# A first-layer product ahead of the counts, and the second block's rows fetched earlier and turned later

## The chip, the cores and the metric

One core of a Trainium2 chip runs the whole program. The metric is the time of one execution in device microseconds; the median of three runs is given, and the profile is of one execution of its own.

## What is computed

Three layers follow one another on 2304 tokens (4 batches of 576) of width 512: a causal attention with a decay, a mixture of eight experts in which each token goes to one expert, and a gated layer. The change lies at the seam of the first two. The reference of these, cut to what matters:

```python
def _attn_ref(q, k, v, f):                     # 4 batches, 8 heads, 576 tokens, width 64
    scores = scale * np.matmul(q, k.transpose(0, 1, 3, 2))
    cum = np.cumsum(np.log(np.clip(f, 0.0001, 1.0)), axis=-1)
    scores = np.where(causal, -1000000000.0, scores + cum[:, :, :, None] - cum[:, :, None, :])
    attn = np.exp(scores - np.max(scores, axis=-1, keepdims=True))
    return np.matmul(attn / (np.sum(attn, axis=-1, keepdims=True) + 1e-09), v)

def _moe_ref(x, w_gate, w_output_gate, w1, w2):
    logits = x @ w_gate
    e_idx = np.argmax(logits, axis=1)          # the one expert of a token
    ...                                        # gate_w: its probability; eom: a sigmoid gate
    for e in range(E):
        mask = e_idx == e
        h = np.maximum(x[mask] @ w1[e], 0.0)
        out[mask] = gate_w[mask, None] * eom[mask, e, None] * (h @ w2[e])
```

## The kernel before

**Attention.** Sixteen pairs of heads (four pairs for each of four batches) are worked on one after another. Every operation of this stage is added to a planner (Flow) with a cost in ns, the engines that may do it, what it reads and writes, and a group, which is the number of its pair. The planner walks a modelled time, takes on each engine the ready operation that can start first and, among equals, that of the earliest group, and emits the instructions in the order so found. In finish (line 444) a pair's output is multiplied by a matrix that holds an identity and the two gates' weights: the product px (L451) has 80 columns for each head, 64 of x and 16 shares of the logits. VectorE scales it by the inverse sums into xb (scale, L461). After the last pair of a batch, logits (line 570) adds the last two heads' shares (L585), and route (line 589) takes the argmax (first, L609 to L614), counts the tokens of each expert by products with a triangle and with ones (prefix, L620 to L625, into the px buffer), works out each token's place in its expert's list (place), and the gate weight (weight, L650). Then the rows, with all 80 columns of 8 heads, are scattered to x_d in DRAM by POOL's indirect DMAs (scatter, L665), five for a batch.

**Before the last batch is known.** While the last pair runs, ahead_rows (line 702) and ahead_steps (line 740) already fetch and turn 216 rows of the expert that leads after three batches, and load and split three of its weight tiles. Every operand of an expert product is split in two: a high half by a cast (ScalarE) and a low half by a subtraction (VectorE); a product is then three matmuls.

**The expert steps.** The function moe (line 996) runs blocks of tokens: block 0 holds those 216 rows, block 1 the next 128 rows of the same expert, block 2 and further the other experts, of up to 336 rows. Each block has eight steps, one for each 128 of the 1024 hidden columns; all steps together are numbered s, so that block 1 begins with step 8 and block 2 with step 16. A step has first products (hidden, L1069, 12 matmuls), a ReLU with its split (relu, L1075 and L1076), and second products (down, L1101 to L1103 or, for 128 rows, L1088 to L1090), which are issued one step later, behind the next step's first products. At a block's end down copies its four outputs (put, L984 and L986: two by ScalarE, two by VectorE). Weight tiles come by SP's DMAs (load, L1014) into a ring of three raw buffers, and split (L1019 and L1020) splits tile s + 2 during step s; load s + 4 is issued in step s, once the split of tile s + 1 has freed its buffer. Rows of the next block are fetched by SP (fetch, L1031), which waits for all scatters, scaled by their gate weight (weigh, L1041 on ScalarE for block 1, L1043 on POOL after that), turned on TensorE (turn, L1053) and split (land, L1057 and L1058). For block 1 the order was: fetch behind load 8 in step 4, weigh at the end of step 6's ReLU, turn and land in step 7, ahead of the second products of step 6 and of the split of tile 9. From here on no planner is at work: each engine has its instructions in the order in which the code issues them, and SP its DMAs.

## Time and profile before

| | us |
|---|---|
| median of 3 runs | 880.24 (880.14 to 880.37) |
| the profiled execution | 880.27 |
| its span, from the first to the last instruction | 878.5 |
| TensorE busy | 851.4 (97% of the span) |
| VectorE busy | 613.2 (70%) |
| ScalarE busy | 451.3 (51%) |
| POOL busy | 316.3 (36%) |

The engines are PE (TensorE), PEld (its weight loads), DVE (VectorE), ACT (ScalarE), POOL and SP, which only issues DMAs here (SPq is its sequencer). L1069 is line 1069 of the kernel. A timeline's row has the start in us from the span's start, the length of the merged stretch, the engine, the line, the operation, out<-in, the shapes and the count; in brackets stands the idle time of the engine before it and what ended that. PEclk is the granted clock of TensorE as a share of 2.4 GHz, averaged over the stretch.

### The profile page before, as it was taken

What the parts mean: (1) busy time and instruction counts of PE and PEld (TensorE: products, weight loads), DVE (VectorE), ACT (ScalarE), POOL (GpSimd) and SP (SyncE); (2) the same over time, 40 slices, a digit from 0 to 9 for tenths busy, and PEclk for the clock granted to TensorE, in tenths of its full rate; (3) what the DMA queues carried; (4) which work ended last, traced back from release to release, by engine and by line L of the source; (5) the groups of instructions that cost most, each with busy time, mean ns of one, the idle gap of its engine ahead of it and who ended that gap; (6) DMA issues with size and microseconds to landing.
All of it is one profiled execution on the core that took longest, in us unless ns stands there. A gap on an engine that the chain in (4) does not pass through costs nothing.

```text
span 878.5 us, 16055 instructions
## 1 busy us (share of the span) xinstructions
PE 851.4 (97%) x5668; PEld 748.8 (85%) x5668; DVE 613.2 (70%) x1435; ACT 451.3 (51%) x990; POOL 316.3 (36%) x382
## 2 busy tenths in 40 slices
PE   7999999998999999999999999999999999999996
PEld 3766667666999999999999898999999989999995
DVE  5777787796675767757747788989898866344444
ACT  5878778785464455546555544353444432332220
POOL 4211233240222231233155346565646285322213
PEclk9999999999999999999999999999999999999999
DMA  7798969552688676687655557777774666655631
GB/s 218 210 294 266 272 195 286 160 175 96 225 265 298 215 249 223 200 298 251 191 175 183 176 187 166 199 149 207 133 185 130 186 227 240 231 205 206 216 131 72
DMA packets 84693, 179.89 MB, mean 205 GB/s; under 512 B 10097, under 2 KB 47473, under 8 KB 83073
## 3 DMA queue, kind: packets, MB, share of 16 engines
q1 hardware_dynamic: 81057, 168.19, 62.2%
q0 software_dynamic: 3552, 10.63, 3.2%
q8 instruction: 46, 0.75, 0.4%
q14 instruction: 38, 0.31, 0.1%
HBM read 123.89 MB, written 54.90 MB: 204 GB/s over the span
## 4 chain that ended last, share of the span: by engine, by line
PE 71%; DVE 9%; DMA 8%; ACT 4%; issue 4%; POOL 3%; SPq 1%; POOLq 0%; ACTq 0%; DVEq 0%
PE po L1505 12%; PE ph L1069 12%; PE w L1415 6%; PE x L1415 6%; PE z L1415 6%; PE py L1101 4%; PE py L1103 4%; PE py L1102 4%; PE y L1415 3%; PE tp L474 3%; PE ps L487 3%; DMA q<-in_qT 2%; PE po L512 2%; PE px L451 1%; DMA k<-in_kT 1%
## 5 line engine op out<-in xcount | busy, mean ns | idle before, releaser
L1433 POOL TENSOR_TENSOR s<-s,s 128x384 f32<-128x384 f32 x36 | 42.9, 1191 | 130.8 <-ACT s L1432 130.7
L1415 PE MATMUL x<-xo,wt 128*128 128x384 f32 x432 | 88.1, 338 | 1.7 <-DVEq L928 0.7
L1415 PE MATMUL z<-xo,wt 128*128 128x384 f32 x432 | 87.1, 335 | 1.9 <-DVE r L1475 1.9
L1415 PE MATMUL w<-xo,wt 128*128 128x384 f32 x432 | 86.7, 335 | 0.3 <-DVE r L1476 0.3
L427 ACT ACTIVATE sc<-sc,nmx 128x512 f32<-128x512 f32 (+3 forms) x128 | 71.7, 563 | 21.6 <-DVE nmx L422 20.7
L1415 PEld LDWEIGHTS x<-xo,wt 128*128 128x128 f32 x432 | 76.5, 188 | 6.4 <-ACT s L1426 1.0
L1415 PEld LDWEIGHTS z<-xo,wt 128*128 128x128 f32 x432 | 76.0, 188 | 3.2 <-DVE r L1475 2.8
L1043 POOL TENSOR_SCALAR xg<-xr 128x512 f32<-128x512 f32 (+5 forms) x20 | 34.9, 1754 | 117.2 <-DMA xr<-x_d 117.2
L1415 PEld LDWEIGHTS w<-xo,wt 128*128 128x128 f32 x432 | 75.9, 188 | 0.6 <-DVE r L1476 0.6
L1238 POOL TENSOR_TENSOR tt<-tt 128x256 f32<-128x256 f32 x48 | 40.2, 849 | 69.0 <-DVE tt L1205 67.6
L1505 PE MATMUL po<-wo,g1h 128*128 128x512 f32 x204 | 64.3, 397 | 0.0
L1426 ACT COPY s<-x 128x384 f32<-128x384 f32 x36 | 17.3, 481 | 90.6 <-PE x L1415 74.4
L345 ACT COPY pt<-tp 128x512 f32<-128x512 f32 (+3 forms) x128 | 50.0, 423 | 14.3 <-PE tp L474 14.1
L474 PE MATMUL tp<-ident,sc 128*128 128x128 f32 x320 | 52.9, 287 | 3.6 <-ACT ptz L345 2.1
L474 PEld LDWEIGHTS tp<-ident,sc 128*128 128x128 f32 x320 | 35.5, 142 | 21.2 <-ACT pt L345 6.5
L487 PE MATMUL ps<-k,q 64*128 64x512 f32 (+3 forms) x256 | 47.1, 476 | 5.7 <-DMA k<-in_kT 5.7
L1511 DVE TENSOR_TENSOR acc<-po,acc 128x512 f32<-128x512 f32 x60 | 39.9, 685 | 16.5 <-PE po L1505 15.8
L422 DVE CUSTOM_DVE_ANT_0 sc<-ps,cm 128x128 f32<-128x128 f32 x128 | 33.2, 285 | 19.6 <-PE tp L474 8.9
L1505 PEld LDWEIGHTS po<-wo,g1h 128*128 128x128 f32 x204 | 38.2, 188 | 7.7
L422 DVE CUSTOM_DVE_ANT_0 sc<-ps,cb,nmx 128x384 f32<-128x384 f32 (+2 forms) x96 | 43.6, 479 | 0.5
L1415 PE MATMUL y<-xo,wt 128*128 128x384 f32 x216 | 43.2, 334 | 0.0
L512 PE MATMUL po<-pt,vt 128*64 128x256 f32 (+1 forms) x384 | 42.1, 350 | 0.0
(334 smaller groups left out, 2436.3 us busy)
## 6 DMA issues: line engine op xcount, KB each, us to landing
raw<-in_w SPq DMA_DIRECT2D x69, 512.0 KB
w_d<-wt SPq DMA_DIRECT2D x84, 256.0 KB
wt<-w_d SPq DMA_DIRECT2D x12, 1792.0 KB
raw<-in_wm SPq DMA_DIRECT2D x18, 1024.0 KB
cb<-cum_d SPq DMA_DIRECT2D x30, 288.0 KB
x_d<-roomf SPq DMA_DIRECT2D x8, 960.0 KB
w_d<-wo SPq DMA_DIRECT2D x24, 256.0 KB
wo<-w_d SPq DMA_DIRECT2D x6, 1024.0 KB
```

The source lines that it names most:

```text
L345: self.nc.scalar.copy(out, in_)
L422: nc.vector.tensor_tensor_reduce(out=sc.t[:, cs], in0=ps.t[:, o:o + w], in1=in1(), scale=-0.125, scalar=acc if c else 3e38, op0=ALU.add, o ...
L427: F.add(lambda e: nc.scalar.activation(sc.t[:, :n], sc.t[:, :n], AF.Exp, bias=nmx.t[:, u:u + 1], scale=-1.0, accum_out=sums.t[:, u:u + 1]) ...
L474: nc.tensor.transpose(tp.t[:n, c - c0], sc.t[:, c * P:c * P + n], self.ident)
L487: nc.tensor.matmul(ps[j].t[:, :ext], lhsT=q.t[h, q0 + 64 * j:q0 + 64 * j + P], rhs=k.t[h, :ext], start=True, stop=True)
L512: nc.tensor.matmul(po.t[64 * j:64 * j + 64, o:w], lhsT=vt.t[:, c, (2 * p + j) * D:(2 * p + j + 1) * D], rhs=at[j].t[:, c, o:w], start=c == ...
L1069: nc.tensor.matmul(ph[:, :n], lhsT=a, rhs=b, start=i == 0, stop=i == len(mm) - 1)
L1238: nc.gpsimd.tensor_tensor(out=ts[:, o], in0=ts[:, a], in1=ts[:, b], op=ALU.subtract)
L1415: nc.tensor.matmul(bank, lhsT=l, rhs=r, start=first and not k and not i, stop=end and k == HK - 1 and i == 2, skip_group_check=True)
L1433: nc.gpsimd.tensor_tensor(out=s5, in0=s5, in1=s7, op=ALU.add)
L1505: nc.tensor.matmul(po, lhsT=a, rhs=b, start=i == 0, stop=i == len(mm) - 1)
L1511: nc.vector.tensor_tensor(out=acc[i], in0=po, in1=acc[i], op=ALU.add)
```

## The change

Step 0's first products become operations of the planner (ahead_hidden), which depend on the last pair's three px products and so come behind them, and have the group of the pair before; its ReLU goes with them, and step 0 of moe has only its second products left. The counts go into the po buffer instead of px. For tiles 0 and 1 of the last pair VectorE scales only the 16 logits' columns of each head; the 64 columns of x are scaled by four ScalarE instructions that the planner puts behind the argmax. In the last batch the logits' additions are done for tiles 2 to 4 and for tiles 0 and 1 apart. In moe the fetch of block 1's rows is issued ahead of load 8; weigh comes behind step 7's ReLU; turn comes behind the second products of step 6, then those of step 7 follow at once, and then land.

```diff
--- before.py
+++ after.py
@@ -450,20 +450,32 @@
                     for h in range(0, n, 64):
                         nc.tensor.matmul(px.t[h:h + 64, i], lhsT=oT.t[:, i * P + h:i * P + h + 64], rhs=self.w2[:, p],
                                          start=True, stop=True)
-            F.add(turn_x, {"PE": 272 * len(ts)}, r=[oT, "w2"], w=[px], group=pr, kind="x", mode="columns")
+            F.add(turn_x, {"PE": 272 * len(ts)}, r=[oT, "w2"], w=[px, ("px", pr, ts[0])], group=pr,
+                  kind="x", mode="columns")
             o = xb[:n, ts[0]:ts[-1] + 1, 2 * p:2 * p + 2, :]
-            x = px.t[:n, 0:len(ts)].rearrange("p t (j c) -> p t j c", j=2)
             w = [("xb", b % 2, p, t) for t in ts]
             if ts[0] < 4:
                 u = [2 * TORD.index(t) + j for t in ts for j in range(2)]

-                def scale(e):
+                def scale(e, cs=slice(0, XW)):
                     nc.vector.tensor_tensor(
-                        out=o, in0=x, op=ALU.mult, in1=rs.t[:, u[0]:u[-1] + 1].rearrange(
-                            "p (t j) -> p t j", j=2).unsqueeze(3).to_broadcast([P, len(ts), 2, XW]))
-                F.add(scale, {"DVE": 70 + 166 * len(ts)}, r=[px] + [(rs, i) for i in u], w=w, group=pr, kind="scale")
+                        out=o[..., cs], in0=px.t[:n, 0:len(ts)].rearrange("p t (j c) -> p t j c", j=2)[..., cs], op=ALU.mult,
+                        in1=rs.t[:, u[0]:u[-1] + 1].rearrange(
+                            "p (t j) -> p t j", j=2).unsqueeze(3).to_broadcast([P, len(ts), 2, cs.stop - cs.start]))
+                ready = [px] + [(rs, i) for i in u]
+                if pr == NP - 1 and ts[0] == 0:
+                    F.add(lambda e: scale(e, slice(D, XW)), {"DVE": 140}, r=ready, w=w + [("xl", b % 2, t) for t in ts], group=pr, kind="scale")
+
+                    def others(e):
+                        for i in range(len(ts)):
+                            for j in range(2):
+                                nc.scalar.activation(o[:, i, j, 0:D], px.t[:n, i, j * XW:j * XW + D], AF.Copy,
+                                                     scale=rs.t[:, u[0] + 2 * i + j:u[0] + 2 * i + j + 1])
+                    self.rest = lambda ohb: F.add(others, {"ACT": 800}, r=ready + [ohb], w=w, group=pr, kind="scale")
+                else:
+                    F.add(scale, {"DVE": 70 + 166 * len(ts)}, r=ready, w=w, group=pr, kind="scale")
             else:
-                F.add(lambda e: self.copy(e, o, x), {"ACT": 190, "DVE": 240}, r=[px], w=w, group=pr, kind="x")
+                F.add(lambda e: self.copy(e, o, px.t[:n, 0:len(ts)].rearrange("p t (j c) -> p t j c", j=2)), {"ACT": 190, "DVE": 240}, r=[px], w=w, group=pr, kind="x")

         def turn(sc, c0, c1, n, out, key):

@@ -581,9 +593,12 @@
                 {"DVE": 570}, r=got, w=[lg], group=pr)
         elif p == NPB - 1:
             lg = self.lg
-            for h in (H - 2, H - 1):
-                F.add(lambda e, h=h: nc.vector.tensor_tensor(out=lg.t, in0=lg.t, in1=xb[:, :, h, D:], op=ALU.add),
-                      {"DVE": 155}, r=got + [lg], w=[lg], group=pr)
+            for t0, t1 in ((2, 5), (0, 2)) if b == B - 1 else ((0, 5),):
+                ready = [("xl", b % 2, t) if b == B - 1 and not t0 else ("xb", b % 2, p, t) for t in range(t0, t1)]
+                for h in (H - 2, H - 1):
+                    F.add(lambda e, h=h, t0=t0, t1=t1: nc.vector.tensor_tensor(
+                        out=lg.t[:, t0:t1], in0=lg.t[:, t0:t1], in1=xb[:, t0:t1, h, D:], op=ALU.add),
+                        {"DVE": 130}, r=ready + [lg], w=[lg], group=pr)
             self.route(b, pr)

     def route(self, b, pr):
@@ -593,7 +608,7 @@
         xb, lg = self.xb[b % 2], self.lg
         sh = [P, 5, E]
         m, m2, ls, ohb, pos, se, so, sel, px = (
-            R[n].new() for n in ("m", "m2", "ls", "ohb", "pos", "se", "so", "sel", "px"))
+            R[n].new() for n in ("m", "m2", "ls", "ohb", "pos", "se", "so", "sel", "po" if b == B - 1 else "px"))
         oh, sli = self.oh[:, b], self.sli[:, b]
         base, nbase = self.base[b], self.base[b + 1]

@@ -613,9 +628,12 @@
             V.tensor_tensor(out=ohb.t, in0=oh, in1=bc(m2.t), op=ALU.is_equal)
             V.memset(ohb.t[64:, 4], 0.0)

+        def counts(t):
+            return t[:, :6 * E] if b == B - 1 else t[:, 0, :6 * E]
+
         def prefix():

-            prf = px.t[:, 0, :6 * E]
+            prf = counts(px.t)
             ohf = ohb.t.rearrange("p t e -> p (t e)")
             nc.tensor.matmul(prf[:, 0:5 * E], lhsT=self.trib, rhs=ohf, start=True, stop=False)
             for t in range(1, 5):
@@ -626,7 +644,7 @@
                                  start=t == 0, stop=t == 4)

         def place():
-            pr3 = px.t[:, 0, :6 * E].rearrange("p (t e) -> p t e", e=E)
+            pr3 = counts(px.t).rearrange("p (t e) -> p t e", e=E)
             V.tensor_tensor(out=pos.t, in0=pr3[:, 0:5], in1=base.unsqueeze(1).to_broadcast(sh), op=ALU.add)
             V.tensor_tensor(out=pos.t, in0=pos.t, in1=ohb.t, op=ALU.mult)
             with nc.allow_low_precision(reason="whole numbers below 2 ** 24"):
@@ -650,6 +668,8 @@
             V.reciprocal(out=xb[:, :, 0, D], in_=se.t)

         add(first, {"DVE": 1200}, [lg], [m, ohb, m2, ("oh", b)])
+        if b == B - 1:
+            self.rest(ohb)
         add(prefix, {"PE": 300}, [ohb, "consts"], [px])
         add(less, {"DVE": 120}, [lg, m], [ls])
         add(lambda: nc.scalar.activation(ls.t, ls.t, AF.Exp), {"ACT": 130}, [ls], [ls])
@@ -760,6 +780,30 @@
                 F.add(lambda e, h=h, l=l, cs=cs, raw=raw: (nc.gpsimd if e == "POOL" else nc.vector).tensor_tensor(
                     out=l, in0=raw[:, cs], in1=h.bitcast(F32), op=ALU.subtract),
                     {"DVE": 600, "POOL": 1230}, r=[("raw", fb), ("wah", fb, i)], w=[("wal", fb, i)], group=g)
+
+    def ahead_hidden(self):
+
+        nc, F = self.nc, self.F
+        g = NP - 2
+        xh, xl = self.xa
+        for s in range(1):
+            (wh, wl), (hh, hl) = self.wa[s], (t[:, :AHEAD] for t in self.ha[s])
+            ps = self.R["ps"].new()
+
+            def mm(e, ps=ps, wh=wh, wl=wl):
+                ms = []
+                for k in range(NK):
+                    a, b = wh[:, k * P:(k + 1) * P], wl[:, k * P:(k + 1) * P]
+                    ms += [(a, xh[:, k]), (a, xl[:, k]), (b, xh[:, k])]
+                for i, (a, b) in enumerate(ms):
+                    nc.tensor.matmul(ps.t[:, :AHEAD], lhsT=a, rhs=b, start=i == 0, stop=i == len(ms) - 1)
+            F.add(mm, {"PE": 1350}, r=[("wah", s, 0), ("wal", s, 0)] + [(x, c) for x in ("xah", "xal") for c in range(2)] + [("px", NP - 1, t) for t in (0, 2, 4)],
+                  w=[ps], group=g)
+            F.add(lambda e, ps=ps, hh=hh: nc.scalar.activation(hh, ps.t[:, :AHEAD], AF.Relu),
+                  {"ACT": 360}, r=[ps], w=[("ha", s)], group=g)
+            F.add(lambda e, ps=ps, hh=hh, hl=hl: nc.vector.scalar_tensor_tensor(
+                out=hl, in0=ps.t[:, :AHEAD], scalar=0.0, in1=hh.bitcast(F32), op0=ALU.max, op1=ALU.subtract),
+                {"DVE": 390}, r=[ps, ("ha", s)], w=[("hl", s)], group=g)

     def attention(self, pool):
         ac, tmp = pool("ac", 1), pool("tmp", 1)
@@ -787,6 +831,7 @@
             if pr < NP:
                 self.attn_operands(pr)
         self.ahead_steps()
+        self.ahead_hidden()
         F.emit()

     def unordered(self, key, ins, behind=None):
@@ -1123,27 +1168,30 @@
             load(s)
         split(NAHEAD)
         for s, (q, fb) in enumerate(steps):
+            if s == 4:
+                fetch(1)
             if s >= NAHEAD - 1:
                 load(s + 1 + NRAW)
-            if s == 4:
-                fetch(1)
             if (q, fb) == (nb - 1, 0):
                 self.most = self.reg(self.nch, E, None, MAXCH)
             nq, c = q + 1, fb - (LATE, 3, 4)[min(q, 2)]
             if s == LATE or fb == 0 and 2 < nq < nb:
                 fetch(max(nq, 2))
             n = len(chunks(nq)) if nq < nb else 0
-            ph = hidden(s)
+            ph = hidden(s) if s else None
             next(offsets, None)
             t = None
-            if 0 <= c < n:
+            if q and 0 <= c < n:
                 t = turn(nq, c)
             early = 1 + (q > 1)
             if q and 0 <= c + early < n:
                 weigh(nq, c + early)
-            relu(s, ph)
-            if not q and 0 <= c + 1 < n:
-                weigh(nq, c + 1)
+            if ph is None:
+                hs[s] = tuple(t[:, :AHEAD] for t in self.ha[s])
+            else:
+                relu(s, ph)
+            if s == LATE:
+                weigh(1, 0)
             next(offsets, None)
             if t:
                 land(*t)
@@ -1162,7 +1210,11 @@
                     next(prep, None)
             if flat:
                 upright(*flat)
-            flat = down(s - 1) if s else None
+            flat = down(s - 1) if s and s != LATE + 1 else None
+            if s == LATE:
+                t = turn(1, 0)
+                down(s)
+                land(*t)
             next(offsets, None)
         down(len(steps) - 1)
         final = self.drops.pop(0)
```

## Rows read from the trace of the kernel before

**Rows 1.** The page, part 1: busy us, share of the span, instructions.

```profile
PE 851.4 (97%) x5668; PEld 748.8 (85%) x5668; DVE 613.2 (70%) x1435; ACT 451.3 (51%) x990; POOL 316.3 (36%) x382
```

**Rows 2.** Windows: length, busy PE, PEld, DVE, ACT, POOL, then PEclk, DMA share, GB/s.

```profile
197.00:199.00 2.00, 1.85 (x12) 1.27 (x14) 1.35 (x7) 1.68 (x8) 0.00 (x0) 1.00 0.66 183
...
213.30:215.90 2.60, 0.10 (x4) 0.06 (x3) 2.11 (x10) 0.00 (x0) 0.00 (x0) 0.97 0.81 331
...
215.90:222.50 6.60, 6.60 (x40) 6.60 (x41) 4.25 (x20) 2.08 (x5) 4.01 (x6) 0.50 0.60 204
...
222.50:225.00 2.50, 2.50 (x24) 2.50 (x24) 0.45 (x2) 0.00 (x0) 2.06 (x4) 0.99 0.96 385
```

**Rows 3.** Timeline of TensorE (start, us, what, [idle before]): the seam, an earlier idle.

```profile
197.15 0.60 PE L474 MATMUL tp<-ident,sc 128*128 128x128 f32 x3 [1.21 <-ACT ptz L345]
...
212.58 0.76 PE L451 MATMUL px<-w,oT 128*64 128x160 f32 x8 [0.52 <-ACT oT L345]
...
215.84 0.21 PE L620 MATMUL px<-ohb,trib 128*128 128x40 bf16 x1 [2.50 <-DVE ohb L614]
...
216.13 0.53 PE L1069 MATMUL ph<-xah,wa0h 128*128 128x216 f32 x1
...
223.29 0.28 PE L1069 MATMUL ph<-xah,wa2h 128*128 128x216 f32 x1
```

**Rows 4.** Timeline of VectorE at the seam.

```profile
213.39 0.49 DVE L461 TENSOR_TENSOR xb<-px,rs 128x320 f32<-128x320 f32 x1 [3.55 <-PE px L451]
...
213.98 0.52 DVE L585 TENSOR_TENSOR lg<-lg,xb 128x80 f32<-128x80 f32 x2
...
214.53 0.20 DVE L609 TENSOR_REDUCE m<-lg 128x5 f32<-128x40 f32 x1
...
217.66 1.23 DVE L1020 TENSOR_TENSOR wl<-raw,wh 128x1024 fp32r<-128x1024 f32 x1
```

**Rows 5.** Chain that ended last (start, us, what): block 0's pitch, a late load.

```profile
231.49 1.34 PE ph L1069 x12
...
234.17 1.34 PE ph L1069 x12
...
239.15 1.06 ACT wa1h L1019
...
241.48 5.99 DMA raw<-in_w
```

**Rows 6.** DMA queues from 227 to 228 (packets, MB, share), then SP's issues.

```profile
q0 software_dynamic: 2, 0.01, 3.1%
...
230.11 0.33 SPq L1014 DMA_DIRECT2D raw<-in_w  x1
...
230.84 0.33 SPq L1031 DMA_DIRECT2D xr<-x_d  x1
```

**Rows 7.** Timeline of TensorE, entry to block 1.

```profile
238.03 0.60 PE L1053 MATMUL tpm<-ident,xg 128*128 128x128 f32 x4
...
239.80 0.23 PE L1069 MATMUL ph<-xh,wa0h 128*128 128x128 f32 x1
...
249.90 0.33 PE L1069 MATMUL ph<-xh,wa0l 128*128 128x128 f32 x1 [0.34 <-DVE wa0l L1020]
```

**Rows 8.** Timeline of ScalarE, entry to block 1.

```profile
235.80 0.71 ACT L1041 ACTIVATE xg<-xr 128x512 f32<-128x512 f32 x1
...
238.23 0.35 ACT L1075 ACTIVATE ha1h<-ph 128x216 fp32r<-128x216 f32 x1 [0.79 <-PE ph L1069]
...
241.51 0.28 ACT L1075 ACTIVATE ha0h<-ph 128x128 fp32r<-128x128 f32 x1 [1.31 <-PE ph L1069]
```

**Rows 9.** Timeline of VectorE, entry to block 1.

```profile
239.29 0.69 DVE L1058 TENSOR_TENSOR xl<-tpm,xh 128x512 fp32r<-128x512 f32 x1
...
240.23 1.23 DVE L1020 TENSOR_TENSOR wa1l<-raw,wa1h 128x1024 fp32r<-128x1024 f32 x1 [0.25 <-ACT wa1h L1019]
...
243.91 0.67 DVE L984 COPY st<-py 128x216 f32<-128x216 f32 x2
```

## The prediction

> **What bounds it now.** I read the engines' busy times first: TensorE is busy 97% of the span [rows 1], so a change pays only where TensorE waits or runs at its lower clock. Next the stretches by window, around the seam between the attention and the expert steps: from 213.3 to 215.9 TensorE does 0.10 us of work, and from 215.9 to 222.5 its granted clock is 0.50, the lower of its levels (1.2 of 2.4 GHz), before it is full again [rows 2]. Then its instructions there [rows 3]: the last attention product px starts at 212.58 and ends at 213.34, the next instruction, the counts at L620, comes at 215.84 after 2.50 us idle, step 0 starts at 216.13, and step 2 at 223.29. The idle time belongs to a chain on VectorE: scaling px, two additions to the logits, the argmax [rows 4]. So the seam has two costs, the idle and the half clock behind it.
>
> Later steps of block 0 are full: twelve first products take 1.34 us, and the pitch of a step is 2.68 [rows 5]. The next place where TensorE waits is the entry to block 1: its step 12 (numbering all steps through) waits at 249.90 for VectorE's split of a weight tile, whose load took 5.99 us to land [rows 5, 7].
>
> **The seam, part by part.** (a) VectorE's chain. Scaling 320 columns takes 0.49, the two additions over 80 columns 0.52 together, and 213.98 + 0.52 puts the argmax at 214.53; the counts start 1.31 after it [rows 3, 4]. After the change 64 columns are scaled; the nearest row is one addition over 80 columns, 0.26, the other end 0.49; I take 0.25. The additions that are left cover 32 columns, between 0 and 0.26 each; I take 0.23. The argmax then starts at 213.39 + 0.25 + 0.46 = 214.10, and the counts at 215.41, 0.43 sooner (bounds 0 and 0.7). The additions for the other three tiles go into VectorE's empty time before 213.39.
>
> (b) Step 0's first products now follow px directly. They need the weights and rows that were split before the last px, and a score buffer free by then. At full clock they end at 213.34 + 1.34 = 214.68, so TensorE idles 0.73 us instead of 2.50 before the counts. What does that to the clock? An idle of 1.21 us at 197.15 left it at 1.00 [rows 2, 3]; 2.50 did not. 0.73 lies below both, so I take the clock as kept.
>
> (c) After the counts (0.29, from 215.84 to 216.13), step 1's first products would start at 215.70. Their accumulator may lie where step 0's was, and that is read last by VectorE's half of step 0's ReLU, queued behind the argmax: 216 columns, by the 0.69 for 512 [rows 9] at most 0.4. I put 0.1 for this wait (0 to 0.4). Step 1 from 215.80, then step 0's second products: 2.68 by [rows 5], so step 2 starts at 218.48 instead of 223.29: **4.8 us sooner**. Of this 0.43 is the shorter chain, 2.68 step 0's products at half clock, and 1.8 the half clock of the products after them, less the 0.1.
>
> (d) ScalarE's four scalings of 64 columns cost at most 4 x 0.28, what 128 columns take [rows 8]. They come after step 0's ReLU, near 215, and end near 216.3; what waits for them are the row scatters, which need VectorE's gate weights too, and those are written just before 217.66 [rows 4]. Without that cover they would delay the scatters by up to 1.1. The counts move to the po buffer, free by then, and px, held until 216.3, is wanted by nobody before the turn: both cost nothing. VectorE gains 0.43 and pays up to 0.4 for the ReLU, so I leave the scatters where they are.
>
> The Trainium skill, "ScalarE: Activation LUTs", section "Rules for kernel authors", speaks against (d): multiply on VectorE, and budget some 0.3 us per ScalarE instruction plus 0.83 ns per element. An estimate by that page is 4 x 0.35 = 1.4 us, which ScalarE's row for 128 columns, 0.28, puts too high [rows 8]; it would still end before 217.66 and change the sum by nothing.
>
> **The entry to block 1.** (e) The fetch of block 1's rows goes ahead of load 8 on SP's queue, by one issue, 0.73 [rows 6]. It used to be issued at 230.84, when the scatters had landed: their queue moves its last two packets between 227 and 228 [rows 6]. Now SP reaches it near 223.5 and stands there; loads 8 and 9 and all later loads queue behind it. Load 7, once sent after the scatters, now shares their time: 0.5 MB at the 385 GB/s of [rows 2] is 1.4 us. So the fetch goes out between 227.1 and 228.6; I take 227.4, since the last packets come that late only because POOL issues them one by one. Load 8 goes 0.73 later. Its landing: no less than its own 1.4, no more than the 5.99 of a load behind block 2's three pieces (0.86 MB) [rows 5]; with 0.33 MB ahead of it instead, 5.99 less 0.53/0.385, or 4.6. It lands near 232.7, where ScalarE wants it at 231. The delay reaches TensorE only through the chain in (f).
>
> (f) The turn of block 1's rows moves from before step 6's second products to behind them, and the splitting of the turned rows (land) now comes after step 7's second products and after the split of weight tile 9, in the queues of ScalarE and VectorE alike. down(7) closes block 0, so its four output copies (two by each) stand ahead of land too. Before: step 7's first products end at 238.03, the turn follows, and step 8 starts at 239.80 with hardly a wait, because the low half xl ran at 239.29, ahead of the weight split at 240.23 [rows 7, 9]. After, with all 4.8 us sooner, step 7's first products end at 233.2; second products of step 6, turn and second products of step 7 (1.35 + 0.38 + 1.38) let TensorE reach step 8 at 236.3. The other side: step 7's ReLU 0.20 after 233.2, 0.35 long; the scaling of the rows, 0.71 [rows 8]; the high half of tile 9, whose low half starts 1.08 behind it (239.15 in [rows 5], 240.23 in [rows 9]) and takes 1.23; two copies, 0.67; xl, 0.69 [rows 9]. That adds up to 238.1: step 8's second product starts then instead of at 236.4, **1.7 us of new wait** (1.0 if the copies were free). Counted from load 8's landing at 232.7 in (e), the same chain with tile 8's high half in front adds up to 238.5; both put durations end to end and so err on the long side, and I stay at 238.1.
>
> (g) Step 8's ReLU comes late with it, and the split of tile 10 follows that ReLU: 0.28 for the ReLU [rows 8], 1.08 and 1.23 for the tile, about 2.5. TensorE has only step 9's first products and step 8's second ones in between, since down(7) no longer lies there: another **0.4 us**. On the other side, before lost 0.5 on the way (0.2 at step 8, whose second product waited for xl until 239.98, and 0.34 at step 12 with its late load [rows 7, 9]), and loads that are wanted later relative to their issue land in time.
>
> Step 12 comes at 249.90 - 4.8 + 1.7 + 0.4 - 0.5, or 246.7: **3.2 us sooner**. From there TensorE's queue is full but for the same small waits as before, so I carry 3.2 to the end.
>
> **The sum.** The profiled execution took 880.27 us (span 878.5 and 1.8 around it), 0.03 above the median of 880.24: 880.27 - 3.2 = 877.1.
>
> **Rivals.** *The late turn costs nothing*: the copies wait for nothing and land slips through, or the load's wait was the true limit of block 1 anyway. All 4.8 stays, and before's 0.5 may go as well: 875.5, at best 875.0. Against it: queues run in order, and the chain in (f) has no free link.
>
> *The clock falls all the same*, in the 0.73 of the seam or, more likely, in the 1.7 us at step 8, which is longer than the 1.21 that kept it and shorter than the 2.50 that did not [rows 3]. Its price is that of [rows 2]: 6.6 us at 0.50, or 3.3 us: 880.4, no change to be measured.
>
> *Step 0's products do not move into the gap* because a buffer or the order holds them behind the counts. Then only the 0.43 is won, the clock falls, and the later turn costs its part: 880.
>
> *Slower: SP stands at the fetch too long.* Each us by which the scatters land after 227.4 delays load 8, tile 8's split, the turned rows and step 8 by one us. With 3.2 to lose, the kernel gets slower from an issue at about 231, and by over 0.2% from 232.5: 882 or more. For it: scatters and loads share engines that were at a DMA share of 0.96 between 222.5 and 225 [rows 2]. Against it: load 7 has only 1.4 us of bytes to put in their way. The Trainium skill, "DMA: Bandwidth & Descriptors", section "Queues, rings and completion order", says that each DMA engine serves the queues with work in turn, packet by packet; by that, load 7 would push the scatters by no more than its own bytes. No row of before has the two together in force.
>
> **How the numbers follow.** Forecast 0.53 (876.1 to 878.4 with the bounds of a, c, e and f); turn free 0.15; clock falls 0.14; products not moved 0.06; slower 0.05; the last 0.07 for an order of the attention that the planner draws up otherwise, as likely up as down. A measurement of this kernel tells 0.2%, or 1.8 us, from no change. Faster: 0.53 + 0.15 + 0.03 + a little of the clock's, 0.74. Same: the clock, the unmoved products and some of the rest, 0.19. Slower: 0.07. The range runs from the free turn, 875.0, to the fallen clock, 880.4, which leaves out about 0.15.
>
> **What would show it.** Right: step 0's products directly behind px, an idle under 1 us before the counts, granted clock 1.00 from there on; step 2 near 218.5; a wait of step 8 for VectorE's xl of 1 to 2 us near 236.5; step 12 near 246.7; the rest shifted by the same 3.2. Wrong: a stretch at 0.50 behind either idle, SP's fetch later than 229, step 8 without a wait, or a shift that shrinks after block 1.

## The result, and the profile after

The change makes the kernel slower: 886.94 us at the median against 880.31, a ratio of 1.0073 with an interval of 1.0051 to 1.0094. The forecast was 877.1, in a range up to 880.4. The profiled execution took 888.52, the longest of the six (883.97 to 888.52), with a span of 886.8 against 878.5.

TensorE's mean granted clock is 0.984 in it, and 0.994 in the profile of before. Page of the changed kernel, part 1: TensorE does the same 5668 products and is busy 8.2 us longer than in [rows 1].

```profile
PE 859.6 (97%) x5668; PEld 755.9 (85%) x5668; DVE 615.4 (69%) x1437; ACT 452.7 (51%) x994; POOL 315.0 (36%) x382
```

The seam is what the forecast says. Timeline of TensorE in the changed kernel, answering to [rows 3]: the last px, step 0's products, the counts, step 1, step 2.

```profile
213.83 0.76 PE L451 MATMUL px<-w,oT 128*64 128x160 f32 x8 [0.52 <-ACT oT L345]
...
214.52 0.37 PE L799 MATMUL ps<-xah,wa0h 128*128 128x216 f32 x1
...
216.66 0.19 PE L638 MATMUL po<-ohb,trib 128*128 128x40 bf16 x1 [0.55 <-DVE ohb L629]
...
216.93 0.35 PE L1114 MATMUL ph<-xah,wa1h 128*128 128x216 f32 x1
...
219.68 0.27 PE L1114 MATMUL ph<-xah,wa2h 128*128 128x216 f32 x1
```

From px to step 2 are 5.85 us, where [rows 3] have 223.29 - 212.58 = 10.71: 4.86 gained, 4.8 forecast. VectorE's chain there, answering to [rows 4]:

```profile
214.64 0.22 DVE L461 TENSOR_TENSOR xb<-px,rs 128x64 f32<-128x64 f32 x1 [3.15 <-PE px L451]
...
214.90 0.42 DVE L599 TENSOR_TENSOR lg<-lg,xb 128x32 f32<-128x32 f32 x2
...
215.35 0.20 DVE L624 TENSOR_REDUCE m<-lg 128x5 f32<-128x40 f32 x1
```

All of that is lost again, and 7.2 us more, between 230 and block 2's first product at 267.18. SP's queue there (DMA issues; L1059 are weight loads, L1076 the fetches of rows), answering to [rows 6]:

```profile
223.86 0.33 SPq L1059 DMA_DIRECT2D raw<-in_w  x1
230.78 0.33 SPq L1076 DMA_DIRECT2D xr<-x_d  x1
231.37 7.12 SPq L1059 DMA_DIRECT2D raw<-in_w  x4
239.21 6.73 SPq L1076 DMA_DIRECT2D xr<-x_d  x3
246.21 0.33 SPq L1059 DMA_DIRECT2D raw<-in_w  x1
```

The fetch of block 1's rows leaves at 230.78, not 227.4, with load 8 behind it. ScalarE waits for that load, with the scaling of the rows queued behind its split. TensorE then waits for the rows at the turn, and for xh and xl at step 8. Timelines of ScalarE and TensorE, answering to [rows 7, 8]:

```profile
235.83 1.04 ACT L1064 CAST wa0h<-raw 128x1024 fp32r<-128x1024 f32 x1 [3.48 <-DMA raw<-in_w]
...
237.02 0.71 ACT L1086 ACTIVATE xg<-xr 128x512 f32<-128x512 f32 x1
```

```profile
237.78 1.12 PE L1098 MATMUL tpm<-ident,xg 128*128 128x128 f32 x4 [1.80 <-ACT xg L1086]
...
241.71 0.33 PE L1114 MATMUL ph<-xh,wa0h 128*128 128x128 f32 x1 [0.33 <-ACT xh L1102]
242.44 0.33 PE L1114 MATMUL ph<-xl,wa0h 128*128 128x128 f32 x1 [0.41 <-DVE xl L1103]
```

The rest is the clock. Windows of the changed kernel (columns as in [rows 2]):

```profile
238.00:241.00 3.00, 3.00 (x15) 3.00 (x15) 2.27 (x7) 1.56 (x3) 0.00 (x0) 0.50 0.56 181
241.00:244.60 3.60, 2.86 (x23) 2.51 (x22) 1.75 (x6) 1.33 (x4) 0.60 (x1) 0.97 0.52 194
244.60:262.00 17.40, 17.40 (x74) 16.24 (x73) 8.82 (x13) 6.69 (x11) 4.81 (x3) 0.51 0.57 188
262.00:266.00 4.00, 4.00 (x33) 3.73 (x32) 2.39 (x5) 2.87 (x5) 0.00 (x0) 1.00 0.40 131
```

For 17.4 us TensorE works without a pause at half its clock, and for 3 us before that. The kernel before, in the same window:

```profile
244.60:262.00 17.40, 17.06 (x124) 15.92 (x123) 12.25 (x19) 10.39 (x18) 4.56 (x3) 1.00 0.77 256
```

124 products there, 74 here. The starts of step 9 and of block 2, in the kernel before and then in the changed one:

```profile
242.69 0.24 PE L1069 MATMUL ph<-xh,wa1h 128*128 128x128 f32 x1
...
258.74 0.32 PE L1069 MATMUL ph<-xh,wa0h 128*128 128x336 f32 x1
```

```profile
243.72 0.28 PE L1114 MATMUL ph<-xh,wa1h 128*128 128x128 f32 x1
...
267.18 0.31 PE L1114 MATMUL ph<-xh,wa0h 128*128 128x336 f32 x1
```

The ledger of the profiled execution, from the starts of the same products in both kernels: px 1.25 later (the attention, see below); the seam -4.86; the entry of block 1 up to step 9 (242.69 before, 243.72 after) +4.64, of which 2.54 are the three waits above and most of the rest half clock; from there to block 2's first product (258.74 before, 267.18 after) +7.41, in which TensorE waits for nothing: half clock. The sum is +8.44; the span grew by 8.3.

### The profile page after: what moved, and what is told of

It reads as the page before. It is cut to its first block, busy times and chain, and to the rows that moved or that the text cites. A ratio compares the mean times of both kernels' runs of the same rounds, so it can differ in the third digit from the quotient of the medians.

```text
span 886.8 us, 16062 instructions
## 1 busy us (share of the span) xinstructions
PE 859.6 (97%) x5668; PEld 755.9 (85%) x5668; DVE 615.4 (69%) x1437; ACT 452.7 (51%) x994; POOL 315.0 (36%) x382
## 4 chain that ended last, share of the span: by engine, by line
PE 71%; DVE 9%; DMA 6%; issue 4%; ACT 4%; POOL 3%; SPq 1%; POOLq 0%; DVEq 0%; ACTq 0%
PE po L1557 12%; PE ph L1114 11%; PE w L1467 6%; PE x L1467 6%; PE z L1467 6%; PE tp L486 4%; PE py L1146 3%; PE y L1467 3%; PE py L1148 3%; PE py L1147 3%; PE po L524 3%; PE ps L499 3%; PE px L451 2%; DMA raw<-in_w 1%; PE tpm L1098 1%
## 5 line engine op out<-in xcount | busy, mean ns | idle before, releaser
L1488 DVE TENSOR_TENSOR s<-y,s 128x384 f32<-128x384 f32 x36 | 19.9, 551 | 32.2 <-PE y L1467 32.2
```

## The experiments

Three theories at the start. Q: SP stands at the early fetch, and the loads behind it are late. T: turning and landing block 1's rows late makes a wait at step 8, by itself or through the clock that falls behind it. S: the moved products disturb the attention. Two came on the way. B: block 2's fetch has three pieces for a ring of three buffers, and load 12 stands behind the third. C is T's second half put by itself: the clock makes the loss. The kernel before's median on the same chip stands beside the first time of each set, and the mean granted clocks of all timed executions beside each time; the kernel before had 0.993 to 0.998 in 81 of 84, and 0.984 to 0.986 with 888 to 890 us in three.

**The two parts apart.** e1 has the seam's part with the expert steps ordered as before; e2 the steps' part with the seam of before, and its edit is shown against the kernel before.

```diff
 e1:        for s, (q, fb) in enumerate(steps):
-            if s == 4:
-                fetch(1)
             if s >= NAHEAD - 1:
                 load(s + 1 + NRAW)
+            if s == 4:
+                fetch(1)
...
-            if s == LATE:
-                weigh(1, 0)
+            if not q and 0 <= c + 1 < n:
+                weigh(nq, c + 1)
...
-            flat = down(s - 1) if s and s != LATE + 1 else None
-            if s == LATE:
-                t = turn(1, 0)
-                down(s)
-                land(*t)
+            flat = down(s - 1) if s else None
 e2 (against the kernel before):
+            if s == 4:
+                fetch(1)
             if s >= NAHEAD - 1:
                 load(s + 1 + NRAW)
-            if s == 4:
-                fetch(1)
...         (weigh, turn, down and land as in the change)
```

> The attention's part of the change alone; in the expert steps the fetch of block 1's rows, their scaling and their turn stay where they were before. Theory Q (SP stands at the fetch, and what is queued behind it comes late): the fetch still waits for the scatters, until about 230, but now holds load 9, not load 8, while ScalarE, in step 6, stands at the scaling of rows that land near 233: 2 to 3 us of wait, a fall of the clock possible, 878 to 885. Theory T (the late turn makes the loss): without it the whole gain of the seam stays, 875 to 876.5. Theory S (the seam itself disturbs the attention and its clock): slower than before, 883 or more.

> The expert steps' part alone: the fetch ahead of load 8 and the late turn, with the seam of before. Theory Q: SP comes to the fetch at 228.6, when the scatters have landed, so nothing waits for it; only the new wait of step 8 for the turned rows is left, 1 to 1.7 us, and 0.4 behind it: 881 to 882.5. Theory T: that wait makes the clock fall as well, 884 to 888. Theory S: nothing lost, 880 to 880.5.

e1: 878.33 against 880.30, ratio 0.9981 (0.9963 to 1.0000), clocks 0.995 to 0.998. e2: 883.84, ratio 1.0025 (0.9988 to 1.0062), clocks 0.988 to 0.996, in seven of its eight executions; the eighth took 3653.83 us at a clock of 1.0, for which no run shows a cause. So the seam's part doesn't make the loss, against S: e1 is no slower than the kernel before. The steps' part does: e1 and the changed kernel differ by it alone, and are 8.6 us apart with intervals that don't meet. By itself, with the seam of before, it is 3.5 us slower at the median, between what Q and T expected, and its interval doesn't tell this from nothing. But the seam alone brings 2.0, not 4.8: the rows of block 1 come from the scatters, which it doesn't make earlier (the last is issued 11.3 us behind px in both kernels). In e1's profile the fetch leaves at 231.30, no sooner than in [rows 6], and TensorE waits for the rows:

```profile
238.40 0.33 PE L1114 MATMUL ph<-xl,wa0h 128*128 128x128 f32 x1 [1.35 <-DVE xl L1103]
```

Counted from px (214.12 in e1, 212.58 before), step 2 is 4.86 us nearer than before, and this product only 3.2 (24.28 against 27.45).

**The fetch and the landing.** e3 puts the fetch behind load 9. e4 does so too, and turns and lands the rows ahead of the last split and of block 0's output copies.

```diff
 e3, e4:
-            if s == 4:
-                fetch(1)
             if s >= NAHEAD - 1:
                 load(s + 1 + NRAW)
+            if s == 5:
+                fetch(1)
 e4:         if s == LATE:
                 weigh(1, 0)
+                down(s - 1)
+                land(*turn(1, 0))
...
-            flat = down(s - 1) if s and s != LATE + 1 else None
-            if s == LATE:
-                t = turn(1, 0)
-                down(s)
-                land(*t)
+            if s == LATE:
+                down(s)
+            else:
+                flat = down(s - 1) if s and s != LATE + 1 else None
```

> The changed kernel with one edit: the fetch of block 1's rows is issued behind load 9 instead of ahead of load 8. Theory Q: loads 8 and 9 go out in time, ScalarE does not stand at load 8, the rows land near 233.5, about when step 7 scales them, and step 8 waits some 1.5 us for its turned rows: 876 to 879, with the clock at full speed. Theory T: the late turn still costs its wait and the clock falls behind it, 883 to 887. Theory S: 884 to 888 as the changed kernel.

> As the one before, and the turned rows are split ahead of the split of weight tile 9 and of block 0's output copies, so that step 8 finds them sooner: the turn still comes behind step 6's second products. Theory Q: step 8's wait shrinks from some 1.5 us to 0.5 or less, 875 to 877. Theory T: the same, 875 to 877, and it differs from the kernel without this edit by more than 6 us. Theory S: 884 to 888.

e3: 882.69, ratio 1.0022 (1.0003 to 1.0041), clocks 0.986 to 0.997. e4: 882.61, ratio 1.0034 (1.0004 to 1.0063), clocks 0.988 to 0.997. Both gain some 4 us on the changed kernel, and neither is where it should be. e4 has no wait of note left at step 8, but a large one at step 12. Its timeline of TensorE, GpSimd's (POOL in the rows) of the same kernel and SP's:

```profile
248.58 0.48 PE L1114 MATMUL ph<-xh,wa0h 128*128 128x128 f32 x1 [3.67 <-ACT wa0h L1064]
249.84 0.47 PE L1114 MATMUL ph<-xh,wa0l 128*128 128x128 f32 x1 [0.57 <-DVE wa0l L1065]
```

```profile
239.86 3.55 POOL L1088 TENSOR_SCALAR xg<-xr 128x512 f32<-128x512 f32 x2 [15.21 <-DMA xr<-x_d]
```

```profile
234.13 8.02 SPq L1076 DMA_DIRECT2D xr<-x_d  x3
242.40 0.33 SPq L1059 DMA_DIRECT2D raw<-in_w  x1
```

The third of block 2's pieces leaves at 241.82, when GpSimd has scaled the first (from 239.86, and the longest of the three scalings is 1.93); in the changed kernel at 245.61, 1.61 behind the start of that scaling at 244.00. In the kernel before the three leave at once:

```profile
239.79 1.38 SPq L1031 DMA_DIRECT2D xr<-x_d  x3
```

By these times the third piece waits for the first one's buffer, since the scaling of block 1's rows, which used to free a buffer ahead of this fetch, now comes behind it. Load 12 stands behind the third piece, and step 12's split behind load 12. That is theory B.

**The buffer, and the clock.** e5 is the changed kernel with a fourth buffer; e6 is e4 with it; e7 is e5 with products that nobody reads in TensorE's waits; e8 is the changed kernel with the fetch ahead of load 7 as well.

```diff
 e5, e6, e7:
-NCH = 3
+NCH = 4
 e7:
+        def fill(n):
+            ph = psH.tile([P, 512], F32, name="ph")
+            for i in range(n):
+                nc.tensor.matmul(ph[:, :P], lhsT=wbuf[LATE % 4][0][:, :P], rhs=xs[0][0][:, 0, :P], start=i == 0, stop=i == n - 1)
...
+            if s == LATE + 1:
+                fill(10)
             ph = hidden(s) if s else None
...
             if s == LATE:
+                fill(20)
                 t = turn(1, 0)
 e8:
-            if s == 4:
+            if s == 3:
                 fetch(1)
```

> The changed kernel with a fourth buffer for fetched rows (NCH = 4), nothing else. In the changed kernel the third piece of the fetch for block two left only when the first piece had been scaled by GpSimd (that scaling began at 244.00 and the piece was issued at 245.61), and load 12 stood behind it until 246.21; in the kernel before all three left at 239.79. Theory B (the ring of three buffers, and load 12 behind it, makes the loss): the third piece leaves within 0.7 us of the second, load 12 at about 241, and the time falls by the 3 to 5 us that the sister kernel with the early landing stood idle at step 12, to 882 to 883. Theory C (TensorE's clock fell after the waits at step 8 and that makes the loss; TensorE was busy throughout from 244 to 262 of the changed kernel, so no load was late for it): the pieces leave as said, the time stays at 885 to 888.

> The changed kernel with the fetch for block one behind load 9, its rows turned and landed ahead of the last split and copies, and a fourth buffer for fetched rows: the run with the early landing, plus the buffer. There step 8 had no wait over 0.35 us, but TensorE stood 3.67 + 0.57 us at step 12 for load 12 (issued 242.40) and worked at half clock for the 6 us behind that. Theory B: load 12 leaves at about 236, step 12 waits under 1 us, the clock stays at 1.00, and the time falls from 882.6 by 4.2 + some 3 to 875.0 to 876.5. Theory C alone also needs no fall of the clock here, since both waits are gone, and gives the same. If another thing costs the time (say the turn ahead of the second-layer products): 880 or more, with no idle at steps 8 and 12.

> The changed kernel with a fourth buffer for fetched rows, and with products that nobody reads put on TensorE while it would wait at step 8: twenty of 128x128 ahead of the turn of block one's rows (1.80 us idle there in the changed kernel) and ten ahead of step 8's first product (0.33 + 0.41 us idle). About 0.08 us each, 1.6 and 0.8 us, so the wait is filled and not shortened. Theory C (the fall of the clock makes the loss): the clock stays at 1.00 from 236 to 262, where the changed kernel had 0.50 for some 20 us, and 877 to 880 comes out. Theory Q (the waits themselves, rows and loads 8 and 9 late, make it): 885 or more whatever the clock.

> The changed kernel with the fetch for block one put ahead of load 7 as well, so that no load runs beside the last scatters. In the changed kernel load 7 left at 223.86, the scatters' last packets ended about 229.5 to 230 (227 in the kernel before), and the fetch left at 230.78 where 227.4 was forecast. Theory S7 (load 7 shares the DMA engines with the scatters and holds them up): the last packets end by about 227.5 and the fetch leaves at 227.5 to 228.5. Rival (the scatters' own length sets it): the fetch leaves at 229.5 or later although no load runs. In both, load 7 leaves only behind the fetch, so step 7 stands for its weights, some 2 to 4 us.

e5: 887.73 against 880.40, ratio 1.0083 (1.0054 to 1.0111), clocks 0.983 to 0.988. The pieces leave together (239.55, 1.39 for all three), load 12 at 241.51, and nothing is gained: for the changed kernel B is not the cause, since TensorE at half clock comes to step 12 later than the load.

e6: 877.41, ratio 0.9958 (0.9931 to 0.9985), clocks 0.993 to 0.999: faster than both kernels, and 0.9 above the upper end of what was expected. The same buffer that is worth nothing in e5 is worth 5.2 us here, between the medians of e4 and e6. The longest wait left in block 1 is 0.62, at 241.76 for tile 10, and the window that had half clock in the changed kernel:

```profile
244.60:262.00 17.40, 17.40 (x122) 16.12 (x122) 12.75 (x18) 12.12 (x20) 0.18 (x1) 1.00 0.78 242
```

e7: 883.67, ratio 1.0025 (0.9989 to 1.0060), and its ten executions fall into two groups: five of 878.48 to 881.97 with clocks of 0.995 to 0.999, five of 885.38 to 887.63 with 0.988 to 0.990. One kernel, one chip: the groups' means are 6.9 us apart, and 0.008 of clock on a span of 880 is 7.0. The first group lies where C had the time, or up to 2 us above; the second, where Q had it, has the lower clock. The profiled execution is of the first group; the waits of the others, and the place where their clock fell, are not recorded. Of e5, which differs by the fill alone, all ten have 0.988 or less. The added products took 0.11 us each (20 in 2.36), not the 0.08 expected. The fill took most of the wait's place, and 0.86 was left. Timeline of TensorE and windows of e7:

```profile
241.16 0.33 PE L1114 MATMUL ph<-xl,wa0h 128*128 128x128 f32 x1 [0.86 <-DVE xl L1103]
```

```profile
234.00:241.00 7.00, 6.29 (x57) 6.15 (x56) 4.14 (x9) 3.92 (x7) 0.00 (x0) 1.00 0.81 289
241.00:262.00 21.00, 20.54 (x150) 19.33 (x151) 14.84 (x25) 13.02 (x22) 5.00 (x3) 1.00 0.77 239
```

e8, one execution: 889.69. The fetch leaves at 227.47, its forecast time. The scatters' queue moved its last packets between 226 and 227 there; in the changed kernel, where load 7 ran beside it, all but its last two before 230. Queue of GpSimd's DMAs (packets, MB, share), e8 from 226 to 227, then the changed kernel from 229 to 230:

```profile
q0 software_dynamic: 37, 0.10, 34.2%
```

```profile
q0 software_dynamic: 45, 0.14, 35.3%
```

As expected the price is paid elsewhere, though it is less than the 2 to 4 us expected at step 7: TensorE waits 0.68 and 0.78 for tile 7 near 233, and 1.77 and 0.82 at step 12, and the clock falls behind both, from 234 and from 254. The last issue of the scatters, first in the changed kernel, then in e8 with its fetch:

```profile
225.14 0.92 POOL L685 DMA_INDIRECT x_d<-xb,sli  x1 [0.21 <-issue]
```

```profile
224.01 0.91 POOL L685 DMA_INDIRECT x_d<-xb,sli  x1 [0.21 <-issue]
...
227.47 0.33 SPq L1076 DMA_DIRECT2D xr<-x_d  x1
```

From this issue to the fetch e8 takes 3.5 us. The five profiles that have the early fetch behind load 7, with the moved seam (the changed kernel, e5, e7, e9, e12), take 5.3 to 6.0.

**More fill, the landing by itself, the steps' part repaired.** e9 fills with 24 and 30 products instead of 20 and 10; e10 is e3 with the fourth buffer; e11 is e6's expert steps behind the seam of before; e12 is e6 with the fetch back ahead of load 8.

```diff
 e9 (from e7):
-                fill(10)
+                fill(30)
...
-                fill(20)
+                fill(24)
 e10 (from e3), e11 (from e2, with the edits of e4):
-NCH = 3
+NCH = 4
 e12 (from e6):
+            if s == 4:
+                fetch(1)
             if s >= NAHEAD - 1:
                 load(s + 1 + NRAW)
-            if s == 5:
-                fetch(1)
```

> As the filled kernel with the fourth buffer, but with 24 products ahead of the turn and 30 ahead of step 8's first product, 0.11 us each (2.6 and 3.3 us). In the first filled kernel VectorE's half of block one's rows (xl) still held TensorE for 0.86 us, and its executions fell into two groups: 878.5 to 882.0 with a mean granted clock of 0.995 to 0.999, and 885.4 to 887.6 with 0.988 to 0.990. Theory C (the time of this change is set by whether the clock falls after the idle times at step 8): no idle over 0.4 us is left there, every execution keeps 0.994 or more, and the median is 879 to 881 although TensorE does 54 products for nothing. If the clock falls for another reason (chance, the other work of these steps): the two groups stay, median 883 or more.

> The changed kernel with the fetch behind load 9 and a fourth buffer for fetched rows, block one's rows still turned and landed behind the second-layer products and the put copies, as the change has it. The late landing is then the only thing left against the run at 877.41: step 8 waits 0.58 + 0.41 us for it. Theory C: that wait starts the fall of the clock in part of the executions, so a spread from 877 to 885 with clocks from 0.998 down to 0.987, and a median of 880 to 883. If the landing costs its wait alone: 878.4 (877.4 + 1.0) and clocks as there, 0.993 to 0.999.

> The kernel before with the steps' part of the change alone, repaired: fetch of block one's rows behind load 9, turned and landed ahead of the last split and copies, a fourth buffer; the seam ahead of it (step 0's products behind the counts) as in the kernel before. Steps' part worth nothing by itself once repaired: 880 to 881, and the 3.0 us of the run at 877.41 are the seam's. Steps' part worth what it was forecast at (block one's turn off the path, 0.9 to 1.0 us): 879.0 to 879.8, and the seam's alone 2.0, as its own run showed (878.33 against 880.3).

> The changed kernel with the early landing and the fourth buffer, but the fetch left ahead of load 8. With three others it makes a square: late landing and early fetch 887.73 (e5), late landing and fetch behind load 9 882.05 (e10), early landing and fetch behind load 9 877.41 (e6), and this one. Theory Q' (the fetch's place costs by itself: rows and load 8 are late, TensorE stands 1 to 2 us near 236 to 238 whatever the landing, and the clock falls behind that in most executions): 882 to 886, clocks of 0.986 to 0.993. If the late landing is the whole cause: 877 to 879 with clocks as in e6, 0.993 to 0.999.

e9: 883.88 against 880.34, ratio 1.0056 (1.0038 to 1.0075), clocks 0.994 to 0.998. The clock is kept in every execution, as theory C has it, with no wait over 0.30 left in the profile. The median is 3 to 5 us above what C expected, and where its rival had it, though the rival's two groups are gone. A part of that is the added products, which lie on the path themselves: step 8 began at 242.44, behind the last 30 of them, and VectorE had finished xl at 240.55, 1.9 us before. Timelines of TensorE and VectorE of e9:

```profile
239.13 3.47 PE L1120 MATMUL ph<-xah,wh 128*128 128x128 f32 x30
```

```profile
239.86 0.69 DVE L1103 TENSOR_TENSOR xl<-tpm,xh 128x512 fp32r<-128x512 f32 x1
```

Against e5, from which it differs by the fill alone, every one of its five times (881.59 to 886.01) is below every one of e5's ten (886.28 to 892.46): with the same order of fetch and landing, and 54 products for nothing.

e10: 882.05, ratio 1.0033 (1.0013 to 1.0054), clocks 0.985 to 0.995. Its waits at step 8 add up to 1.06 us; against e6 it loses 4.6. Timeline of TensorE and windows:

```profile
238.25 0.33 PE L1114 MATMUL ph<-xh,wa0h 128*128 128x128 f32 x1 [0.58 <-ACT xh L1102]
239.06 0.33 PE L1114 MATMUL ph<-xl,wa0h 128*128 128x128 f32 x1 [0.48 <-DVE xl L1103]
```

```profile
236.00:240.50 4.50, 3.44 (x30) 3.12 (x27) 2.80 (x6) 1.73 (x4) 0.00 (x0) 1.00 0.92 296
240.50:251.00 10.50, 10.50 (x49) 9.82 (x48) 5.06 (x9) 4.13 (x8) 5.63 (x3) 0.54 0.71 226
```

e11: 880.31, ratio 0.9999 (0.9985 to 1.0013), clocks 0.993 to 0.997. Repaired, the steps' part is worth nothing without the seam: there the rows are early enough anyway. Behind the moved seam it is worth the 0.9 from e1's 878.33 to e6's 877.41, which the two intervals don't tell apart.

e12: 880.35 against 880.28, ratio 1.0005 (0.9988 to 1.0022), clocks 0.988 to 0.998, between its two expectations. TensorE waits 2.03 us for the rows at the turn, works at half clock for 3.6 us, and then, with nothing to wait for at step 8, keeps its clock:

```profile
237.40:241.00 3.60, 3.55 (x18) 3.56 (x18) 2.67 (x7) 2.11 (x4) 0.00 (x0) 0.53 0.63 189
241.00:262.00 21.00, 20.58 (x150) 19.08 (x150) 15.62 (x27) 12.42 (x21) 5.14 (x3) 1.00 0.83 260
```

Four kernels, all with four buffers and the moved seam, make a square (us):

| | fetch ahead of load 8 | fetch behind load 9 |
|---|---|---|
| rows landed late | 887.73 (e5) | 882.05 (e10) |
| rows landed early | 880.35 (e12) | 877.41 (e6) |

The late landing costs 7.4 or 4.6, the early fetch 5.7 or 2.9. Both edits of the steps' part harm, each by itself and more together; by the ratios to the kernel before, the two add up (1.25% together, 0.75% and 0.47% alone). In the profiles both do it through the same two things: a wait at the entry of block 1, and the half clock behind it. The profiles of e5 and e10 have a fall of the clock in the attention as well, 1.7 us each (mean clock 0.81 from 194 to 203), those of e6 and e12 have none. How often it came in the other executions is not recorded, so a part of the square's differences may be its; the smallest of them, 2.9, is more than 1.7.

## Why the prediction was wrong

(a) to (c), the seam: right. The counts start 2.83 after px instead of 3.26, the forecast 0.43 sooner. The scaling took 0.22 (0.25 forecast), the additions 0.42 (0.46 for the two that were left), the idle before the counts 0.55 (0.73), the granted clock stayed at 1.00 from 219 to 235, step 2 came 4.86 nearer to px. The ReLU of step 0 runs on VectorE behind the argmax chain, at 216.64, and step 1 didn't wait for it.

(d) Right: ScalarE's four scalings took 0.92 together, at 216.40, at most 1.12 forecast, and the gate weights came after them.

(e) Wrong, and the first term to fail. The issue at 227.4, with bounds to 228.6, came at 230.78. Of the 3.4 us, 1.2 are the scatters' own start: their last issue was at 225.14, 223.91 in the profile of before, because px was 1.25 later. The other 2.2 are load 7. From the last issue to the fetch are 230.78 - 225.14 = 5.6 us in the changed kernel and 227.47 - 224.01 = 3.5 in e8, without load 7; with four more profiles on the one side it is 1.9 to 2.5 that load 7 costs. I allowed 1.2 for it at the upper bound and next to nothing in the value taken. The sentence of the Trainium skill that I set beside it ("DMA: Bandwidth & Descriptors", "Queues, rings and completion order") has each engine serve the queues in turn, by which, as I read it, load 7 would cost the scatters no more than its own 1.4 us; the measured 2.2 is more, and decides. Load 8's landing was sized well: 4.46 after its issue, 4.6 forecast.

Not seen at all: the third piece of block 2's fetch. I counted SP's queue for the fetch that is moved and not for the one that it is moved past. The scaling of block 1's rows goes behind the fetch of block 2; four pieces then share three buffers. In the changed kernel that is hidden, as e5 shows; in e4 it costs about 5 us.

(f) Right in mechanism, short in size, and wrong in place: 1.7 us of new wait were forecast at step 8, and 0.33 + 0.41 were measured there. The larger part, 1.80, lay at the turn, which itself had to wait for the rows, because the issue was late. The chain from load 8's landing to step 8's second product took 6.6 us (235.83 to 242.44), 5.8 in my sum.

(g) and the sum: here the forecast broke. I gave the fall of the clock 0.14 and the price of [rows 2], 3.3 us, and the late issue 0.05, as cases that exclude each other. They came together, the late issue with the wait behind which the clock fell, and the clock's price at block 1 was 7.4 us behind step 8 and some 1.5 more behind the turn (3.00 us at 0.50). The two idles that I compared with, 1.21 that kept the clock and 2.50 that did not, bound nothing: in the changed kernel's own attention the same 1.21 was followed by half clock. The row to price the fall from was not the seam's 6.6 us at 0.50; how long the half clock lasts was an unknown that the one row could not bound, and the slower side of the range should have stayed open. By the rival's own rule an issue at 230.78 would have left the time about even; the fall of the clock took it to 0.7% worse. The 0.4 for tile 10's split was right in size: e7 and e9, which kept the clock in their profiles, wait 0.30 there.

The gain that I put on the seam was too large as well, even had all else gone right. e1 has the 4.8 us at step 2 and keeps 2.0: the rows of block 1 hang on the scatters, which I left in place in (d) without asking what that does to the rest of the gain. What the seam could bring is e1's 2.0, and with the steps arranged for it e6's 3.0.

What stays open is the attention. In the profiled execution px is 1.25 us later, with the instructions of TensorE and GpSimd up to it in the same order; VectorE has one of the moved additions more there, and on ScalarE one copy (ptt) stands two places earlier, shortly before px. The clock fell there, behind idle times of 1.03 and 1.21, and the fall cost 1.7 us (mean clock 0.81 from 194 to 203). Window of the changed kernel:

```profile
197.40:200.20 2.80, 2.80 (x12) 2.04 (x13) 1.23 (x6) 1.96 (x7) 0.00 (x0) 0.50 0.62 200
```

The profile of e2, which has the seam of before, shows the same fall, so the moved products are not needed for it. But px began at 212.3 to 214.9 in the eleven profiles with the moved seam (mean 213.4), and at 211.4 to 213.6 in the three without (mean 212.5): a small cost of theory S is neither shown nor excluded.

## What to carry to other kernels

When TensorE's work is moved forward, look for what the next stage takes from elsewhere (here rows that are scattered and fetched): the gain ends there. Moving a fetch ahead in a queue moves every later load behind its wait, and moving the reader of a buffer past the next fetch takes a buffer from that fetch; count both. A wait of one microsecond on a TensorE that is otherwise full is priced with a fall of the clock, as a case on the slower side whose length is not known. Filling such a wait kept the clock here (e9), but the filling cost time of its own; what paid was to remove the wait (e6: fetch behind load 9, rows landed early, a fourth buffer).

## What the runs showed of the hardware

The length of an idle time alone doesn't tell whether the clock falls. In e1's profile TensorE stood 1.35 us at step 8, and its clock stayed at 1.00 from 216 to 270; all ten of its executions have 0.995 to 0.998. In e10's it stood 0.58 + 0.48 at the same place and the clock fell; five of its seven executions have 0.985 to 0.990. In the attention, of the eight profiles with idle times of 1.02 to 1.38 and 1.21 close together five fell (the changed kernel, e2, e3, e5, e10) and three did not (e1, e6, e7); of the six others, with no more than one idle time over 0.7 there, none fell. The Trainium skill, "TensorE: Matmul & The Clock Gate", section "What's actually happening", says that the count of slow products at a kernel's start varies from run to run for one kernel. e7's two groups differ from run to run too, though their difference is not known to lie at the start, and no run here shows whether the reason is the same.

Nor does a full queue bring the clock back soon: TensorE was busy 17.40 of 17.40 us at 0.51 in the changed kernel's block 1 and 10.50 of 10.50 at 0.54 in e10's, while behind the turn the half clock was over after some 3 us in the changed kernel and 3.6 in e12. What sets this length is not shown. And a load of 0.5 MB that ran beside the last scatters put their end back by 1.9 to 2.5 us (five profiles against e8's one), more than the 1.4 that its bytes take at the rate of [rows 2].
